# Moving the weight loads behind the first evicted keys, and reordering the first item's steps, in a block-sorted attention and mixture kernel

## The chip, the cores and the metric

The kernel runs on one core of one Trainium2 chip. The metric is device time in microseconds (us), the median of three runs. The profile is one execution of the same program; its span counts from the first to the last recorded instruction and is about 2 us shorter than the time, since it leaves out the start and the end of the launch.

## What is computed

For four batch items (B), eight heads (H), 768 positions (S) and 64 dimensions (D), the sequence is cut in 8 blocks of 96 positions. A small 8x8 matrix per head is normalised five times by rows and columns (Sinkhorn), and its rows mix the blocks of the keys and of the values. Then each block of queries attends to its own mixed block. The result, 3072 tokens of 512, goes through a layer with two first matrices whose products are compared by element, and an output matrix.

```
for _ in range(5):
    P = P - np.max(P, axis=-1, keepdims=True)
    P = np.exp(P)
    P = P / (np.sum(P, axis=-1, keepdims=True) + 1e-09)
    P = P / (np.sum(P, axis=-2, keepdims=True) + 1e-09)
k_sorted = np.einsum('bhij,bhjcd->bhicd', P, k_b)
v_sorted = np.einsum('bhij,bhjcd->bhicd', P, v_b)
scores = scale * np.matmul(q_b, k_sb.transpose(0, 1, 2, 4, 3))
attn = softmax(scores)
x = np.matmul(attn, v_sb)
out = np.maximum(x @ w1, x @ w2) @ w_out
```

The kernel uses max(a, b) = relu(a - b) + b: it forms W1 - W2 once (w_difference), computes relu(x(W1 - W2)) Wout, and adds x(W2 Wout), with the product W2 Wout computed once on the chip.

## The kernel before, in words

Each engine gets its instructions in the order in which the program text issues them, and runs them in that order. Waits between engines are semaphores that the language sets from the data. PSUM is one pool of four buffers of 4 KB per partition; every group of matmuls takes one and holds it until its eviction by VectorE (DVE) or ScalarE (ACT).

The start: TensorE (PE) runs matmuls of zeros (keep_streaming, line 82), so that its clock is up when work arrives, while DVE and ACT run the Sinkhorn rounds. There are 86 zero matmuls of 126 columns, and in the last two rounds six more of 512 columns each, which wait for a small memset of that round (late_zeros). Meanwhile GpSimd (POOL) issues all loads on one queue, with a cast from float32 to bf16: v of the first item in three pieces, k in three, q in four, then W2 and W1 by columns (lines 767 to 773), Wout, and k of the second item. An issue waits until the eighth load before it has landed. Between these POOL builds selection matrices (selections) and later computes W1 - W2 for two of the four column blocks (w_difference on lines 775 and 776); DVE does the other two (diff2 and diff3 below). ACT and DVE copy v into another order (turn_v).

Then the first item's steps, the string `front` (lines 783 to 789), is read from left to right. A step is one group of PE matmuls and its eviction:

- k0 to k2: the keys' mixing, a third each, into kT (sort_k, line 458). v0 to v3: the values' mixing, a quarter each, into v_sb (sort_v, line 479). tq0 and tq1: transposes of the queries (line 433).
- SC0 to SC7: scores of one group of heads and half the blocks (line 548), then exp on ACT into a tile e (line 556). They need all three k steps and one of the tq steps: SC0, SC1, SC4 and SC5 need tq0, the others tq1.
- VA0 to VA7: attention times values (line 575), which need that e and all four v steps; DVE then divides by the sums (lines 586 and 592) into x.
- tx0 to tx3: transposes of x (line 613). tw0 and tw1: transposes of halves of W2 (line 638). h..a and h..b: the two halves of x(W1 - W2) for a half of the tokens and a column block (line 677); the b half is evicted with the relu.
- F0 and the like: the next step's group is led by one zero matmul of 512 columns. pe2 makes the mixing matrices of the other items.

A letter at the end, A or D, fixes the engine that evicts; ACT evicts an h step without one. The first step, k0, is led by two zero matmuls of 320 columns. Behind the front come the other items, woven into the layer of the item ahead of them, and the output.

Of the kernel before, what the change touches and what calls it, by code (L numbers as in the profile page):

```python
# [11 lines left out]
BF16 = mybir.dt.bfloat16  # L12
# [4 lines left out]
def kernel(  # L17
# [16 lines left out]
    nc = tc.nc  # L34
# [4 lines left out]
    B, H, S, D = q.shape  # L39
    NB = sort_net.shape[-1]  # L40
    BLK = S // NB
    G = B * H
# [12 lines left out]
    const = ctx.enter_context(tc.tile_pool(name="const", bufs=1))  # L55
# [10 lines left out]
    def ps_f32(name):  # L66
        return psum.tile([128, 1024], FP32, tag="ps", name=name)
# [9 lines left out]
    def keep_streaming(ps, n, by=None, most=512):  # L77

        w0 = fill[:, 0:128] if by is None else late[by]
        while n > 0:  # L80
            w = min(n, most)
            nc.tensor.matmul(ps[:, 0:w], w0, fill[:, 0:w], start=True, stop=True)  # L82
            n -= w
# [35 lines left out]
    kT = {}  # L119
# [7 lines left out]
    for n in range(NE):  # L127
        t = big.tile([BLK, 8 * BLK + 32], BF16, tag=f"e{n}", name=f"e{n}")
# [23 lines left out]
    def load_k(b):  # L152
        k_raw[b] = (
            kpool.tile([128, HB * D], BF16, tag="k_raw", name="k_raw")
            if b < 3
            else v_raw[:, 0 : HB * D]
        )
        n = HB * D // NCH
        for ci in range(NCH):
            nc.gpsimd.dma_start(  # L160
                out=k_raw[b][:, ci * n : (ci + 1) * n],
                in_=k_src[b, :, ci * n : (ci + 1) * n],
            )
# [10 lines left out]
    w1_sb = big.tile([128, HP, DFF], BF16, tag="w1", name="w1_sb")  # L174
    w2_sb = big.tile([128, HP, DFF], BF16, tag="w2", name="w2_sb")
    wo_sb = big.tile([128, NFB, DMODEL], BF16, tag="wo", name="wo_sb")

    def load_w(dst, src):
        s = src.rearrange("(t p) f -> p t f", p=128)
        n = s.shape[1] // 2  # L180
        for i in range(2):
            nc.gpsimd.dma_start(
                out=dst[:, i * n : (i + 1) * n, :], in_=s[:, i * n : (i + 1) * n, :]
            )

    def load_w_columns(dst, src, t0, t1):
        s = src.rearrange("(t p) f -> p t f", p=128)
        c = slice(t0 * DFF // 4, t1 * DFF // 4)
        nc.gpsimd.dma_start(out=dst[:, :, c], in_=s[:, :, c])
# [13 lines left out]
    def selections(b, eng=nc.gpsimd):  # L203
        heads = {0: (0, 1), 2: (2, 1), 3: (3, 3)}.get(b)
        if heads:
            sel_v[b] = const.tile([G, 2, 8, NB], BF16, tag=f"sel_v{b}", name="sel_v")
            for half, item in enumerate(heads):
                eng.tensor_copy(
                    out=sel_v[b][:, half],
                    in_=ident[0:G, item * 8 : item * 8 + 8].to_broadcast([G, 8, NB]),  # L210
                )
        if b == 0:
            return
        sel_k[b] = const.tile([G, 8, 16], BF16, tag=f"sel_k{b}", name="sel_k")
        eng.tensor_copy(
            out=sel_k[b], in_=ident[0:G, b * 8 : b * 8 + 8].to_broadcast([G, 8, 16])
        )
# [11 lines left out]
    def w_difference(t, eng=None):  # L229
        n = DFF // 4  # L230
        (eng or nc.vector).tensor_tensor(
            out=w1_sb[:, :, t * n : (t + 1) * n],
            in0=w1_sb[:, :, t * n : (t + 1) * n],
            in1=w2_sb[:, :, t * n : (t + 1) * n],
            op=ALU.subtract,
        )
        if not eng:
            load["D"] += 600
# [3 lines left out]
    def turn_v(rows, eng, c0, c1):  # L242
        dst, src = v_dc[rows, 0 : D * BLK], v_raw[rows]
        if eng == "A":
            nc.scalar.copy(
                out=dst.rearrange("p (d c two) -> p d c two", c=BLK, two=2)[:, :, c0:c1],
                in_=src.rearrange("p (c d two) -> p d c two", c=BLK, two=2)[:, :, c0:c1],
            )
        else:
            nc.vector.tensor_copy(  # L250
                out=dst.bitcast(U32).rearrange("p (d c) -> p d c", c=BLK)[:, :, c0:c1],
                in_=src.bitcast(U32).rearrange("p (c d) -> p d c", c=BLK)[:, :, c0:c1],
            )
# [98 lines left out]
    def block_diagonals_first():  # L352

        pe = ps_f32("pe")
        for j in range(NB):
            nc.tensor.matmul(
                pe[:, 0:NB],
                one_j[:, j * 128 : (j + 1) * 128],
                p_bf[:, :, j],
                start=(j == 0),  # L360
                stop=(j == NB - 1),
            )
        nc.tensor.matmul(
            pe[:, 512:576],
            sel_v[0].rearrange("g two h j -> g (two h j)"),
            p_bf.rearrange("p i j -> p (i j)"),
            start=True,
            stop=True,
        )
        bd = const.tile([128, 8, NB], BF16, tag="bd10", name="bd")  # L370
        nc.vector.tensor_tensor(
            out=bd,
            in0=maskM[:, 1].to_broadcast([128, 8, NB]),
            in1=pe[:, 0:NB].to_broadcast([128, NB, 8]).transpose([0, 2, 1]),
            op=ALU.mult,
        )
        bd_k[0] = bd.rearrange("p m i -> p (m i)")
        pm = const.tile([128, NB, NB], FP32, tag="pm1", name="pm")
        nc.vector.tensor_tensor(
            out=pm,  # L380
            in0=pe[:, 512:576].rearrange("p (i j) -> p i j", j=NB),
            in1=maskJ[:, 0].to_broadcast([128, NB, NB]).transpose([0, 2, 1]),
            op=ALU.mult,
        )
        pt = const.tile([128, NB], FP32, tag="pt1", name="pt")
        nc.vector.reduce_sum(out=pt, in_=pm, axis=AX.X)
        bd = const.tile([128, 8, NB], BF16, tag="bd00", name="bd")
        nc.vector.tensor_tensor(
            out=bd,
            in0=maskM[:, 0].to_broadcast([128, 8, NB]),  # L390
            in1=pt.to_broadcast([128, NB, 8]).transpose([0, 2, 1]),
            op=ALU.mult,
        )
        bd_v[0] = bd.rearrange("p m i -> p (m i)")
# [355 lines left out]
        return SC, VA, TR  # L750

    first, second, both = slice(0, 64), slice(64, 128), slice(0, 128)
    keep_streaming(ps_f32("fill_ps"), 86 * 126, most=126)
    for it in range(5):
        sinkhorn(it)
        if it < 3:
# [5 lines left out]
    for c, n, m in [(2, 2, 0), (4, 3, 1)]:  # L762
        nc.gpsimd.tensor_copy(
            out=maskJ[:, c : c + n],
            in_=maskJ[:, m].to_broadcast([128, NB, n]).transpose([0, 2, 1]),
        )
    for t in range(2):
        load_w_columns(w2_sb, moe_w2, t, t + 1)
        load_w_columns(w1_sb, moe_w1, t, t + 1)
    for b in range(1, B):  # L770
        selections(b)
    load_w_columns(w2_sb, moe_w2, 2, 4)
    load_w_columns(w1_sb, moe_w1, 2, 4)
    load_w(wo_sb, moe_w_out)
    w_difference(0, nc.gpsimd)
    w_difference(1, nc.gpsimd)
    load_k(1)
    turn_v(first, "A", 36, 56)
    turn_v(first, "A", 56, 80)
    block_diagonals_first()  # L780
    turn_v(first, "D", 80, 96)

    front = """
        k0D k1A k2D v1D v2A v3A tq0D v0A tq1D SC1 SC0 F1
        SC2 VA1 SC5 VA0 SC3 F2 VA2 SC4 F0 tx0D SC6 VA3
        SC7 h00a VA4 tx1A tw0D h01a VA5 h01bA diff2 h00bA VA7 tx2A
        tw1A h02a VA6 h02bA h11a diff3 tx3A h12a h03a h12bD h10a h10bA
        pe2 h11bD h03bA h13a h13bA
    """.split()
    fills = [0]  # L790

# [4 lines left out]
    def front_step(step):  # L796

        eng = step[-1] if step[-1] in "AD" else None
        name = step[:-1] if eng else step
        kind = name.rstrip("0123456789ab")  # L800
        n = [int(x) for x in name if x.isdigit()]
        if kind == "F":
            fills[0] = 512
        elif kind == "k":
            sort_k(0, n[0], 640 if step == front[0] else 0, eng)
        elif kind == "v":
            sort_v(0, n[0], 0, eng)
        elif kind == "tq":
            q_transposes(0, n[0], eng)
        elif kind == "SC":  # L810
            scores(0, n[0], fills_due())
        elif kind == "VA":
            values(0, n[0], fills_due())
        elif kind == "tx":
            x_transposes(0, n[0], eng)
        elif kind == "tw":
            w2_transposes(n[0], eng)()
        elif kind == "diff":
            w_difference(n[0])
        elif kind == "pe":  # L820
            block_diagonals([(0, 2), (0, 3), (1, 1), (1, 2), (1, 3)], 2)
        elif name[-1] == "a":
            moe_h_products(0, n[0], n[1], (0, 2), fills_due())
        else:
            moe_h(0, n[0], n[1], eng, (1, 3))

    for step in front[:-26]:
        front_step(step)

    load_q(1)  # L830
# [131 lines left out]
```

The softmax here doesn't subtract the row's maximum and nothing guards it: scores larger than these inputs give would overflow.

## Time and profile before

| what | value |
|---|---|
| time, median of three (lowest, highest) | 166.7 us (166.54, 166.72) |
| span of the profile | 164.7 us |
| PE busy | 159.5 us (97%) |
| DVE, ACT, POOL busy | 76.4, 83.1, 32.7 us |
| PE idle before its first matmul | 1.2 us |
| first mixing of keys starts at | 12.21 us |
| second item's mixing of keys starts at | 38.24 us |

The share of PE tells that it is busy nearly everywhere, zero matmuls included: their 7.8 us at the start are PE time that does no work. Between the last two rows of the table stands the whole first item.

### The profile page before, as it was taken

The numbers are of one execution on the slowest core, as the hardware profiler recorded it, in microseconds if no ns is written. First come the engines' busy times: TensorE is split into PE (matmuls) and PEld (weight loads), VectorE is DVE, ScalarE is ACT, GpSimd is POOL, SyncE is SP. The second block draws the span as 40 slices with busy tenths as digits, with TensorE's granted clock in tenths as the row PEclk, the third lists the DMA queues.
The fourth block names the chain that finished last, engine by engine and source line by source line (L and its number), as shares of the span: only waits on it lengthen the run. The fifth ranks groups of instructions, "written<-read, shape, count | busy, mean of one in ns | idle before, by whom it ended". The sixth has DMA issues, their size and how long they took to land.

```text
span 164.7 us, 4563 instructions
## 1 busy us (share of the span) xinstructions
PE 159.5 (97%) x2018; PEld 96.6 (59%) x2018; DVE 76.4 (46%) x169; ACT 83.1 (50%) x102; POOL 32.7 (20%) x59
## 2 busy tenths in 40 slices
PE   7999899999999999999999999999999999999992
PEld 7958678756554555557655554575655546554451
DVE  5869778556375564535277863250642320000011
ACT  3585995918139846055652262557447206642020
POOL 7989687150104000000014010000000000000000
PEclk9999999999999999999999999999999999999999
DMA  3999999999999995688425999991025293000333
GB/s 51 200 204 197 199 208 205 210 204 220 207 205 211 218 232 108 175 116 210 98 31 97 186 193 227 184 229 12 0 52 175 50 179 128 0 0 0 127 131 128
DMA packets 30404, 23.90 MB, mean 145 GB/s; under 512 B 16752, under 2 KB 25200, under 8 KB 30384
## 3 DMA queue, kind: packets, MB, share of 16 engines
q0 software_dynamic: 11040, 13.37, 48.4%
q1 hardware_dynamic: 19200, 10.17, 26.2%
q8 instruction: 16, 0.26, 0.6%
q10 hardware_dynamic: 144, 0.07, 0.1%
q14 instruction: 4, 0.03, 0.1%
HBM read 26.75 MB, written 6.29 MB: 201 GB/s over the span
## 4 chain that ended last, share of the span: by engine, by line
PE 93%; DVE 3%; ACT 1%; issue 1%
PE out_ps L704 38%; PE h_ps L677 26%; PE fill_ps L82 6%; PE o_ps L575 5%; PE wc_ps L657 4%; PE s_ps L548 4%; PE k_ps L458 3%; PE tq_ps L433 2%; DVE kT L110 1%; PE v_ps L523 1%; PE tw_ps L638 1%; ACT e L556 1%; PE tx_ps L613 1%; PE v_ps L500 1%; DVE qT L110 1%
## 5 line engine op out<-in xcount | busy, mean ns | idle before, releaser
L704 PE MATMUL out_ps<-wo_sb,g 128*128 128x512 bf16 (+2 forms) x200 | 48.3, 371 | 0.1
L677 PE MATMUL h_ps<-xT,w_sb 128*128 128x384 bf16 x256 | 44.5, 326 | 0.0
L677 PEld LDWEIGHTS <-w_sb 128*128 128x128 bf16 x256 | 24.0, 98 | 15.6
L556 ACT ACTIVATE e<-s_ps 96x768 bf16<-96x768 f32 x32 | 23.9, 804 | 13.6 <-PE s_ps L548 13.3
L691 ACT ACTIVATE g<-h_ps 128x768 bf16<-128x768 f32 x27 | 21.8, 811 | 17.4 <-PE h_ps L677 17.3
L704 PEld LDWEIGHTS <-g 128*128 128x128 bf16 x200 | 17.1, 97 | 15.8
L704 PE MATMUL out_ps<-wc,xT 128*128 128x512 bf16 (+2 forms) x100 | 24.8, 370 | 0.0
L108 ACT COPY o<-out_ps 128x1024 f32<-128x1024 f32 x10 | 10.1, 1012 | 28.0 <-PE out_ps L704 25.2
L592 DVE TENSOR_TENSOR x<-o_ps,rs 96x512 bf16<-96x512 f32 x32 | 22.0, 687 | 1.1
L704 PEld LDWEIGHTS <-xT 128*128 128x128 bf16 x100 | 9.6, 97 | 11.2
L575 PEld LDWEIGHTS <-e 96*128 96x128 bf16 x256 | 11.8, 97 | 5.9 <-DVE v_sb L110 0.2
L586 DVE RECIPROCAL rs<-o_ps 96x8 f32<-96x8 f32 x32 | 6.4, 201 | 17.7 <-PE o_ps L575 17.5
L739 DVE COPY o<-out_ps 128x512 f32<-128x512 f32 (+1 forms) x2 | 1.2, 625 | 27.6 <-PE out_ps L704 27.6
L575 PE MATMUL o_ps<-v_sb,e 96*128 96x65 bf16 x256 | 12.9, 193 | 0.0
L110 DVE CAST kT<-k_ps 128x1024 bf16<-128x1024 f32 x7 | 8.3, 1215 | 9.4 <-PE k_ps L458 9.4
L108 ACT CAST v_sb<-v_ps 96x1024 bf16<-96x1024 f32 x10 | 9.8, 1013 | 2.5 <-PE v_ps L479 0.9
L693 DVE TENSOR_SCALAR g<-h_ps 128x768 bf16<-128x768 f32 x5 | 4.8, 956 | 10.8 <-PE h_ps L677 10.8
L110 DVE CAST v_sb<-v_ps 96x1024 bf16<-96x1024 f32 x6 | 7.3, 1217 | 5.1 <-PE v_ps L523 2.2
L160 POOL DMA_DIRECT2D v_raw<-in_k_dram x3 | 2.5, 839 | 35.2 <-DVE v_dc L250 31.4
L548 PEld LDWEIGHTS <-kT 64*128 64x128 bf16 x256 | 6.1, 94 | 5.5 <-issue 3.6
L548 PE MATMUL s_ps<-qT,kT 64*128 64x96 bf16 x256 | 8.6, 204 | 0.7 <-PE o_ps L575 0.4
L82 PE MATMUL fill_ps<-fill 128*128 128x126 bf16 x86 | 7.8, 280 | 1.2 <-DVE fill L73 1.2
(95 smaller groups left out, 143.5 us busy)
## 6 DMA issues: line engine op xcount, KB each, us to landing
out_dram<-o SPq DMA_DIRECT2D x11, 512.0 KB, 3.1
v_raw<-in_v_dram POOLq DMA_DIRECT2D x8, 384.0 KB, 12.7
k_raw<-in_k_dram POOLq DMA_DIRECT2D x9, 256.0 KB, 9.9
w_sb<-in_moe_w_dram POOLq DMA_DIRECT2D x4, 256.0 KB, 9.2
w_sb<-in_moe_w_dram POOLq DMA_DIRECT2D x2, 512.0 KB, 10.6
wo_sb<-in_moe_w_out_dram POOLq DMA_DIRECT2D x2, 512.0 KB, 14.4
v_raw<-in_v_dram POOLq DMA_DIRECT2D x3, 256.0 KB, 4.6
q_raw<-in_q_dram POOLq DMA_DIRECT2D x4, 192.0 KB, 8.8
```

The lines of the kernel that those rows point to most:

```text
L82: nc.tensor.matmul(ps[:, 0:w], w0, fill[:, 0:w], start=True, stop=True)
L108: nc.scalar.copy(out=out_ap, in_=in_ap)
L110: nc.vector.tensor_copy(out=out_ap, in_=in_ap)
L548: nc.tensor.matmul(ps[:, h2 * 512 + ii * 128 : h2 * 512 + ii * 128 + BLK], kT[b][rows, (hp * 8 + i) * BLK : (hp * 8 + i) * BLK + 128], rhs ...
L556: nc.scalar.activation(out=e[:, 0 : 8 * BLK].rearrange("p (t c r) -> p t c r", t=8, r=R), in_=ps[0:BLK] .rearrange("p (t f) -> p t f", t=8 ...
L575: nc.tensor.matmul(ps[:, h2 * 512 + ii * 65 : h2 * 512 + (ii + 1) * 65], e[:, (h2 * 4 + ii) * BLK : (h2 * 4 + ii) * BLK + 128], v_sb[:, m0 ...
L586: nc.vector.reciprocal(out=rs, in_=ov[:, :, :, 64])
L592: nc.vector.tensor_tensor(out=x, in0=ov[:, :, :, 0:D], in1=rs.to_broadcast([BLK, 2, 4, D]), op=ALU.mult,)
L657: nc.tensor.matmul(ps[:, 0:512], w2T[:, fb, dmt * 128 : (dmt + 1) * 128], wo_sb[:, fb, :], start=(fb == 0), stop=(fb == NFB - 1),)
L677: nc.tensor.matmul(h_ps[ch, t][:, m * 512 : m * 512 + TCH], w1_sb[:, hp, fb * 128 : (fb + 1) * 128], xT[:, b % 2, ch, hp % 2, hp // 2, :], ...
L691: nc.scalar.activation(out=g, in_=src, func=AF.Relu)
L704: nc.tensor.matmul(dst, g_tiles[b, ch, m // 2][:, m % 2, off : off + 128] if m < NFB else xT[:, b % 2, ch, hp % 2, hp // 2, off : off + 12 ...
```

## The change

Three things change together. The loads of W2, W1 and Wout, the two w_difference steps of POOL and the load of the second item's keys are issued on POOL only after the first piece of keys has been mixed and evicted: a two-column copy of kT into a small tile `seen` makes POOL wait for that. Another such copy, of the Sinkhorn result p_bf, stands ahead of the selection matrices of the other items, which move in front of the weight loads. The order of the first item's steps is another one, with other evicting engines and four F marks in place of three. And the zero matmuls at the start become 92 of 118 columns. The aim is to keep the weight traffic away from the loads and the engines' work that the first item needs, with an order of steps that suits the later weights.

```diff
-    keep_streaming(ps_f32("fill_ps"), 86 * 126, most=126)
+    keep_streaming(ps_f32("fill_ps"), 92 * 118, most=118)
...
-    for t in range(2):
-        load_w_columns(w2_sb, moe_w2, t, t + 1)
-        load_w_columns(w1_sb, moe_w1, t, t + 1)
-    for b in range(1, B):
-        selections(b)
-    load_w_columns(w2_sb, moe_w2, 2, 4)
-    load_w_columns(w1_sb, moe_w1, 2, 4)
-    load_w(wo_sb, moe_w_out)
-    w_difference(0, nc.gpsimd)
-    w_difference(1, nc.gpsimd)
-    load_k(1)
     turn_v(first, "A", 36, 56)
     turn_v(first, "A", 56, 80)
     block_diagonals_first()
+    seen = const.tile([128, 2, 2], BF16, tag="seen", name="seen")
+    nc.gpsimd.tensor_copy(out=seen[0:G, 0], in_=p_bf[:, NB - 1, NB - 2 :])
+    for b in range(1, B):
+        selections(b)
     turn_v(first, "D", 80, 96)
 
     front = """
-        k0D k1A k2D v1D v2A v3A tq0D v0A tq1D SC1 SC0 F1
-        SC2 VA1 SC5 VA0 SC3 F2 VA2 SC4 F0 tx0D SC6 VA3
-        SC7 h00a VA4 tx1A tw0D h01a VA5 h01bA diff2 h00bA VA7 tx2A
-        tw1A h02a VA6 h02bA h11a diff3 tx3A h12a h03a h12bD h10a h10bA
-        pe2 h11bD h03bA h13a h13bA
+        k0A k1D k2A v1A v2D v0A tq0D F0 v3D SC1 SC0 tq1D
+        SC4 F2 VA1 SC5 F1 VA0 SC3 SC2 VA4 tx0D SC7 F3
+        VA3 VA2 SC6 tw0D h00a tx1A tw1A VA5 diff3 diff2 h01a h00bA
+        h01bA tx2A h03a VA6 h03bA VA7 h02a h13a tx3D h02bD h12a h13bA
+        pe2 h12bD h10a h11a h10bA h11bA
     """.split()
...
-    for step in front[:-26]:
+    front_step(front[0])
+    nc.gpsimd.tensor_copy(out=seen[:, 1], in_=kT[0][:, 0:2])
+    for t in range(2):
+        load_w_columns(w2_sb, moe_w2, t, t + 1)
+        load_w_columns(w1_sb, moe_w1, t, t + 1)
+    load_w_columns(w2_sb, moe_w2, 2, 4)
+    load_w_columns(w1_sb, moe_w1, 2, 4)
+    load_w(wo_sb, moe_w_out)
+    w_difference(0, nc.gpsimd)
+    w_difference(1, nc.gpsimd)
+    load_k(1)
+    for step in front[1:-26]:
         front_step(step)
```

## The prediction, made before the changed kernel had run

> **What bounds the kernel now.** I read the page first. Its first part has PE busy for 97% of the span, and the chain of waits goes through PE:
>
> ```profile
> PE 159.5 (97%) x2018; PEld 96.6 (59%) x2018; DVE 76.4 (46%) x169; ACT 83.1 (50%) x102; POOL 32.7 (20%) x59
> ...
> PE 93%; DVE 3%; ACT 1%; issue 1%
> ```
>
> Asked by stretches, PE was busy 11.16 of the 12 us from 12 to 24, then 14.00 of 14 (24 to 38), 25.87 of 26 (38 to 64) and 50.00 of 50 (64 to 114). So a microsecond is won or lost only before 24 us, unless the change opens a new wait later. Then the timeline of PE, where the first item stands:
>
> ```profile
> 1.20 7.76 PE L82 MATMUL fill_ps<-fill 128*128 128x126 bf16 x86 [1.20 <-DVE fill L73]
> 8.80 2.75 PE L82 MATMUL fill_ps<-fill,late 128*128 128x512 bf16 x12
> 11.48 0.37 PE L356 MATMUL pe<-p_bf,one_j 32*128 32x8 bf16 x8
> ...
> 12.21 1.71 PE L458 MATMUL k_ps<-bd,k_raw 64*64 64x64 bf16 x96
> ...
> 18.01 0.52 PE L548 MATMUL s_ps<-qT,kT 64*128 64x96 bf16 x16
> 18.45 0.39 PE L82 MATMUL s_ps<-fill 128*128 128x512 bf16 x1
> 19.13 0.35 PE L548 MATMUL s_ps<-qT,kT 64*128 64x96 bf16 x8 [0.28 <-DVE qT L110]
> ...
> 20.25 0.34 PE L548 MATMUL s_ps<-qT,kT 64*128 64x96 bf16 x8 [0.42 <-PE o_ps L575]
> ...
> 23.56 0.82 PE L677 MATMUL h_ps<-xT,w_sb 128*128 128x384 bf16 x4
> ```
>
> The reader should see that the fills run without a gap into the first real matmul at 11.48, that the scores start at 18.01, and that two idle stretches (0.28 and 0.42 us) and the zero matmuls between the scores are what is left to win. From 23.56 on, PE has no gap until the second item at 38.24.
>
> POOL's timeline and the loads' landing times say how late the weights may be:
>
> ```profile
> 9.46 2.34 POOL L189 DMA_DIRECT2D w_sb<-in_moe_w_dram  x3
> 12.36 0.74 POOL L189 DMA_DIRECT2D w_sb<-in_moe_w_dram  x1 [0.56 <-DMA k_raw<-in_k_dram]
> ...
> 19.22 2.12 POOL L231 TENSOR_TENSOR w_sb<-w_sb 128x1024 bf16<-128x1024 bf16 x1 [1.56 <-DMA w_sb<-in_moe_w_dram]
> 21.94 2.13 POOL L231 TENSOR_TENSOR w_sb<-w_sb 128x1024 bf16<-128x1024 bf16 x1 [0.59 <-DMA w_sb<-in_moe_w_dram]
> ```
>
> The first weight load, issued at 9.46, lands 8.2 us later (17.7), while the very first load of the kernel, issued at 1.24, lands after 4.0. The other 4 us are its place in the queue: q's last piece, issued at 7.2, lands after 9.0 (16.2).
>
> **What the Trainium skill says.** "DMA: Bandwidth & Descriptors", section "Two DMAs through the same engine are not ordered", says that descriptors of one queue start in order, although they need not finish in it. The trace agrees as to landings: v, k, q, W2, W1 and Wout land in the order of issue. So weights queued behind q take nothing from q, and issuing them later should not bring q or k forward. "TensorE: Matmul & The Clock Gate", section "Back-to-back issue gap", gives N/1.2 ns for N columns while the clock is low and N/2.4 + 2.5 when it is up. For 126 columns that is 105 and 55 ns; the trace's 86 fills take 7.60 us from 1.20 to 8.80, which is 57 at 105 and 29 at 55, and the count of fills per 0.4 us indeed rises from 7 to 12 near 7.2 us. "SBUF — State Buffer", section "Who interferes with whom", says that a DVE copy in a two-port mode and a GpSimd instruction exclude each other. The turn_v copy of DVE at 12.72 (0.67 us) beside POOL's issue at 12.36 may show it, but nothing in the trace separates the two.
>
> **The change, part by part.**
>
> *Zero matmuls.* 92 of 118 columns are 10,856 columns against 10,836. If columns set the time, the clock rises again about 6.0 us after the start, 61 of them run at 98 ns and 31 at 51.7, and the end moves from 8.80 to 8.82. If each fill had a fixed price (7.60/86 = 88 ns), it would move by 6 x 88 = 0.53 us, and all of it would count, since the twelve late fills behind them end only at 11.37 while p_bf is ready at 11.07. I take 0.02: v's mixing loads 128 columns of weights per matmul of 64 and needs 34 ns per pair (48 in 1.65 us), so loading does not set the price of a fill.
>
> *Later weight loads.* POOL now waits for p_bf (11.07), copies it, makes the selections (1.6 us from 13.10 to 14.69 in the trace, now from 11.4 to 13.0), waits for kT, then issues. The k0 eviction goes to ACT, which is free at 12.21: matmuls 12.21 to 12.76, eviction 12.9 to 13.9. With the small copy the first weight issue is at 14.3 in place of 9.46. The queue has run out of q at about 14.8 and first packets follow an issue by 1.7 us (1.24 to 2.95 for v), so the queue stands empty for about 1.2 us. The first W2 piece lands between 18.3 (14.3 + 4.0) and 18.8 instead of 17.7: all weights, and everything queued behind them, come 0.6 to 1.1 us later. Six W issues of 0.74 and two Wout of 0.75 keep POOL until 20.25; its two differences end at 22.4 and 24.5 (before: 21.34 and 24.07). Who waits for them: tw0 at 23.7 needs the third piece (about 21.0 to 21.5); h00a at 24.6 needs the first difference (22.4); tw1 at 25.6 needs the fifth piece (24.3 before, now 24.9 to 25.4); diff3 on DVE at 27.8 needs the sixth (26.9 before, now 27.5 to 28.0; h03a follows at 29.1 only); h01a at 26.8 needs the second difference (24.5). Later, k of item 2 lands at 35.7 + 1.1 = 36.8 at the latest and is used from 38.2; Wout by 33.4, used at 40; the queries by 41.5, used at 43.4; the first halves of v by 45.1, used by turn_v at 45.2; the second halves by 49.2, used at 48.9, with the mixing of v at 51.8 behind a turn_v that ended at 50.42. So PE should not feel any of it, by margins of 0.2 to 2 us. I take zero; the upper end is 0.5 us if the pieces come twice as late as estimated.
>
> *The new order.* I stepped the four queues forward by hand through both strings, with the durations of the timeline: per step on PE 0.55 (k, v), 0.80 (tq), 0.22 to 0.28 (SC), 0.24 (VA, or 0.35 ahead of SC), 0.34 (tx), 0.90 (tw), 0.66 and 0.65 (h), and evictions of 1.01 and 1.22 (k, on ACT and DVE), 0.98 and 1.20 (v), 0.96 (tq), 0.81 (exp), 0.93 (reciprocal and multiply), 0.54 or 0.80 (tx), 1.23 or 1.87 (tw), 0.81 or 0.96 (h), with the four PSUM buffers as the program assigns them. For the string of before this ends the front at 38.01 (the trace: 38.24). For the new one:
>
> - k1 is evicted on DVE from 13.45 (behind turn_v), v2 from 15.1 to 16.3, tq0 from 16.6 to 17.56. So SC1 starts at 17.6, 0.4 us earlier than 18.01, and ACT, with the last v eviction done at 16.9, starts the exps at 17.9 in place of 18.39.
> - Then DVE has v3 (to 18.7) and tq1 (to 19.9) ahead of the first division: VA1 starts at 19.3 (19.41 before), VA0 with its fill waits for tq1's buffer and starts at 20.2 (20.52), tx0 waits 0.34 for the second division and starts at 21.7 (21.99).
> - VA3 with its fill waits 0.36 for the exp of SC2, the sixth in line (17.9 + 6 x 0.77 = 22.5), and starts at 22.8; VA2, SC6 and tw0 follow, h00a at 24.6.
> - From there no wait over 0.12. The front ends at 38.12.
>
> The waits and zero matmuls inside the front are 1.34 + 0.65 us in the old order and 1.42 + 0.86 in the new one; about 0.19 comes back because fewer VA groups stand ahead of an SC. Net +0.11. The score start gained is lost again at VA0, tx0 and VA3, and one more zero matmul (0.22) is paid.
>
> *The seen copies* cost POOL 0.3 us each, and POOL idles there otherwise. If a selection copy and turn_v exclude each other, turn_v ends up to 0.3 later and k1's eviction with it, which v2's (0.4 us of idle on DVE ahead of it) takes up.
>
> Sum: 0.02 + 0 + 0.11, about 0.1 us: 166.7 + 0.1 = 166.8 us.
>
> **The rivals.**
>
> 1. Faster. The pause of 0.42 us at 20.25 before has no releaser that explains it (the named o_ps group belongs to another buffer, and my stepping has SC5 at 19.8), and all of the gain of 0.4 at the scores could last until h00a if the divisions run closer than I stepped them. Against it: the new order puts 5 evictions on DVE ahead of the first division. It would give 166.7 - 0.5 = 166.2 us.
> 2. Slower, by DVE: v3 and tq1 hold back the first division, the four buffers fill, and PE waits 0.3 more at each of VA0 and tx0: 166.8 + 0.6 = 167.4 us. For it: the two longest waits I step are of this kind.
> 3. Slower, by weights: the empty queue costs 2 us in place of 1; tw1 then waits 0.7 and diff3 0.9, of which PE sees about 0.7: 167.5 us. For it: tw1's margin is 0.2 to 0.7. Against it: W's place in the queue was behind q in any case.
>
> **How the numbers follow.** No change (within 0.33 us of before) 0.41, since the sum is 0.1 and the stepping missed the known order by 0.23; rival 1 0.27; rival 2 0.2 and rival 3 0.12, together 0.32. The range runs from 165.9 (rival 1 with the second half of its reserve, another 0.3) to 167.5 (rivals 2 and 3); beyond lies the 0.53 of the fills on top of them.
>
> **What would show it.** Right: fills end within 0.05 us of 8.80; the first score at 17.5 to 17.7; the first W issue near 14.3 and the first difference near 20.3; h00a at 24.4 to 24.9; second item's k mixing at 38.2 to 38.5; PE without gaps after it. Wrong: a wait on w_sb ahead of tw1 or h01a, a late fill start near 9.3, a gap at 49 to 52 us behind turn_v, or a front that ends before 37.9 or after 38.6.

## The result and the profile after

| what | before | after |
|---|---|---|
| time, median (lowest, highest) | 166.62 us (166.15, 166.72) | 167.52 us (167.21, 167.77) |
| span of the profile | 164.7 us | 165.8 us |
| first mixing of keys starts at | 12.21 us | 11.93 us |
| second item's mixing of keys starts at | 38.24 us | 39.29 us |
| from there to the end of the span | 126.46 us | 126.51 us |

The changed kernel takes 1.0059 times as long, with a 95% interval of 1.0033 to 1.0085: it is slower by 0.9 us, where the forecast was no change. The last row tells where to look. What follows the second item's first matmul is as long as before, so all of the loss lies in the first 39 us.

The page of the changed kernel, its busy times and then its chain of waits (shares of the span), answers the first lines shown of the kernel before:

```profile
PE 159.4 (96%) x2025; PEld 96.4 (58%) x2025; DVE 77.3 (47%) x170; ACT 82.4 (50%) x101; POOL 33.3 (20%) x61
...
PE 82%; DMA 7%; DVE 5%; POOL 2%; ACT 2%; issue 1%
PE out_ps L704 37%; PE h_ps L677 25%; DMA w_sb<-in_moe_w_dram 6%; PE wc_ps L657 4%; PE o_ps L575 4%; PE k_ps L458 3%; PE s_ps L548 3%; POOL w_sb L189 2%; PE v_ps L523 1%; DMA p_sb<-in_sort_net_dram 1%; DVE v_dc L250 1%; PE tq_ps L433 1%; DVE colsum L276 1%; DVE p_sb L273 1%; PE tw_ps L638 1%
```

PE's work is the same to 0.1 us, but PE's share of the chain fell from 93% to 82%, and the DMA of w_sb, which had no part that was shown before, now has 6%, with POOL's issues of it at 2% (L189). Somewhere the weights have become the last to arrive. The timeline of PE (start, duration, group, and in brackets the idle time and its releaser) says where:

```profile
1.20 7.31 PE L82 MATMUL fill_ps<-fill 128*128 128x118 bf16 x92 [1.20 <-DVE fill L73]
8.34 2.75 PE L82 MATMUL fill_ps<-fill,late 128*128 128x512 bf16 x12
...
11.93 1.84 PE L458 MATMUL k_ps<-bd,k_raw 64*64 64x64 bf16 x96
...
17.29 0.52 PE L548 MATMUL s_ps<-qT,kT 64*128 64x96 bf16 x16 [0.16 <-DVE qT L110]
...
24.13 0.81 PE L677 MATMUL h_ps<-xT,w_sb 128*128 128x384 bf16 x4
24.78 0.51 PE L613 MATMUL tx_ps<-ident,x 96*128 96x96 bf16 x8
26.76 1.07 PE L638 MATMUL tw_ps<-ident,w_sb 128*128 128x128 bf16 x16 [1.48 <-DMA w_sb<-in_moe_w_dram]
...
39.29 1.70 PE L458 MATMUL k_ps<-bd,k_raw 64*64 64x64 bf16 x96
```

The line of 26.76 is tw1, the transposes of the second half of W2. PE stands still for 1.48 us ahead of it, for the fifth piece of the weights, the second half of W2. Up to there the new order is no worse than the old: the scores start at 17.29 in place of 18.01, the bracket of 0.42 us at 20.25 is gone, and h00a runs at 24.13, where I had stepped 24.6.

Of the 0.72 us at the scores, 0.28 is the earlier first mixing, which differs as much between profiles with the same zero matmuls. These 92 zero matmuls took 7.31 us here, and 7.78 and 6.25 in two of the experiments below (tw1 put later, and the new order with the loads at their old place):

```profile
1.20 7.78 PE L82 MATMUL fill_ps<-fill 128*128 128x118 bf16 x92 [1.20 <-DVE fill L73]
1.20 6.25 PE L82 MATMUL fill_ps<-fill 128*128 128x118 bf16 x92 [1.20 <-DVE fill L73]
```

In the six profiles with this form, one matmul takes 99 ns at first and 52 later, and the step comes at 3.9 us in one profile and at 7.2 in another. The first mixing starts between 11.90 and 12.21 us accordingly, so a difference of 0.3 us in a single pair of profiles tells nothing of the kernels.

POOL's timeline answers the lines shown of before and tells why the piece is late:

```profile
11.23 0.18 POOL L771 COPY seen<-p_bf 32x2 bf16<-32x2 bf16 x1 [1.76 <-DVE p_bf L278]
...
13.73 0.19 POOL L821 COPY seen<-kT 128x2 bf16<-128x2 bf16 x1 [0.49 <-ACT kT L108]
13.97 4.45 POOL L189 DMA_DIRECT2D w_sb<-in_moe_w_dram  x6
18.37 1.53 POOL L182 DMA_DIRECT2D wo_sb<-in_moe_w_out_dram  x2
21.24 2.12 POOL L231 TENSOR_TENSOR w_sb<-w_sb 128x1024 bf16<-128x1024 bf16 x1 [1.34 <-DMA w_sb<-in_moe_w_dram]
```

The first issue comes at 13.97 in place of 9.46, close to the 14.3 of the prediction. By the trace, the first weight piece then lands at 19.08 (before: 17.69), the third at 22.45 (20.51), the fifth at 26.71 (24.34) and the sixth at 29.32 (26.94). The last piece of q had landed at 16.86 (16.36). The delay is 1.4 us at the first piece, 2.0 at the second (21.10 in place of 19.08) and 2.4 from the fifth on, so most of it is made before 21 us. The two kernels by stretches (busy time and count of each engine, then PE's clock, the packets in flight on the DMA engines, as a multiple of their number of sixteen, and KB moved per us), first before:

```profile
15.00:16.00 1.00, 0.96 (x30) 0.79 (x28) 1.00 (x2) 0.76 (x1) 1.00 (x2) 1.00 1.43 197
16.00:17.00 1.00, 1.00 (x36) 0.91 (x33) 1.00 (x2) 1.00 (x2) 1.00 (x3) 1.00 1.44 195
17.00:18.00 1.00, 1.00 (x34) 0.86 (x30) 0.72 (x1) 0.83 (x2) 0.66 (x1) 1.00 1.50 210
18.00:19.00 1.00, 0.84 (x21) 0.56 (x18) 0.88 (x1) 0.94 (x2) 0.00 (x0) 1.00 1.40 187
19.00:20.00 1.00, 0.70 (x16) 0.49 (x15) 0.21 (x2) 1.00 (x3) 0.78 (x1) 1.00 1.47 196
```

and after:

```profile
15.00:16.00 1.00, 1.00 (x33) 0.88 (x31) 1.00 (x1) 1.00 (x2) 1.00 (x2) 1.00 0.75 101
16.00:17.00 1.00, 1.00 (x27) 0.69 (x21) 0.80 (x2) 0.65 (x1) 1.00 (x3) 1.00 1.27 170
17.00:18.00 1.00, 0.84 (x27) 0.73 (x28) 1.00 (x2) 0.33 (x1) 1.00 (x2) 1.00 0.89 90
18.00:19.00 1.00, 1.00 (x31) 0.74 (x26) 0.72 (x2) 1.00 (x2) 1.00 (x2) 1.00 1.16 137
19.00:20.00 1.00, 1.00 (x23) 0.72 (x22) 0.97 (x3) 1.00 (x3) 0.91 (x2) 1.00 1.09 132
```

The last column is the one to read. Before, these five microseconds move 985 KB (197 + 195 + 210 + 187 + 196). After, they move 630 KB. The missing 355 KB are 1.8 us of transfer at 197 KB per us. Only a part of it is the empty queue that I had foreseen. From 15 to 16 us, where q runs out and the first weight packets come (15.42), 96 KB are missing. From 17 to 20 us 234 KB are missing: the rate is 90 to 137 there, and the packets in flight are 0.89 to 1.16 in place of 1.40 to 1.50.

### The profile page after: what moved, and what is told of

The parts are those of the page before. It is cut to its first block, busy times and chain, and to the rows that moved or that the text cites. A ratio compares the mean times of both kernels' runs of the same rounds, so it can differ in the third digit from the quotient of the medians.

```text
span 165.8 us, 4579 instructions
## 1 busy us (share of the span) xinstructions
PE 159.4 (96%) x2025; PEld 96.4 (58%) x2025; DVE 77.3 (47%) x170; ACT 82.4 (50%) x101; POOL 33.3 (20%) x61
## 4 chain that ended last, share of the span: by engine, by line
PE 82%; DMA 7%; DVE 5%; POOL 2%; ACT 2%; issue 1%
PE out_ps L704 37%; PE h_ps L677 25%; DMA w_sb<-in_moe_w_dram 6%; PE wc_ps L657 4%; PE o_ps L575 4%; PE k_ps L458 3%; PE s_ps L548 3%; POOL w_sb L189 2%; PE v_ps L523 1%; DMA p_sb<-in_sort_net_dram 1%; DVE v_dc L250 1%; PE tq_ps L433 1%; DVE colsum L276 1%; DVE p_sb L273 1%; PE tw_ps L638 1%
## 5 line engine op out<-in xcount | busy, mean ns | idle before, releaser
L677 PEld LDWEIGHTS <-w_sb 128*128 128x128 bf16 x256 | 24.0, 98 | 15.5
L110 DVE CAST kT<-k_ps 128x1024 bf16<-128x1024 f32 x6 | 7.2, 1222 | 10.0 <-PE k_ps L458 9.9
L110 DVE CAST v_sb<-v_ps 96x1024 bf16<-96x1024 f32 x7 | 8.5, 1219 | 4.8 <-PE v_ps L523 2.8
L108 ACT CAST v_sb<-v_ps 96x1024 bf16<-96x1024 f32 x9 | 8.8, 1009 | 1.4 <-PE v_ps L500 0.8
L169 POOL DMA_DIRECT2D v_raw<-in_v_dram x11 | 5.9, 541 | 13.3 <-DVE v_dc L250 7.7
## 6 DMA issues: line engine op xcount, KB each, us to landing
v_raw<-in_v_dram POOLq DMA_DIRECT2D x8, 384.0 KB, 14.3
```

The source lines that it names most:

```text
L108: nc.scalar.copy(out=out_ap, in_=in_ap)
L110: nc.vector.tensor_copy(out=out_ap, in_=in_ap)
L169: nc.gpsimd.dma_start(out=v_raw[r0 : r0 + 64, m * n : (m + 1) * n], in_=v_src[b, :, m * n : (m + 1) * n],)
L677: nc.tensor.matmul(h_ps[ch, t][:, m * 512 : m * 512 + TCH], w1_sb[:, hp, fb * 128 : (fb + 1) * 128], xT[:, b % 2, ch, hp % 2, hp // 2, :], ...
```

## The experiments

Two questions stood open. First, is the wait of tw1 the whole loss, and does it come from the place of the loads or from the order of the steps? I call the theory that the loads' place alone loses the time W; its rivals lay it on the order or on the zero matmuls. Second, what was the pause of 0.42 us at 20.25, which is gone in the changed kernel? Each ratio below is against the kernel before, with its 95% interval.

**The new order with the loads at their old place.** The changed kernel, with the loads, selections and differences put back at their old place and neither of the two copies:

```diff
+    for t in range(2):
+        load_w_columns(w2_sb, moe_w2, t, t + 1)
...
     turn_v(first, "A", 36, 56)
...
     front_step(front[0])
-    nc.gpsimd.tensor_copy(out=seen[:, 1], in_=kT[0][:, 0:2])
-    for t in range(2):
-        load_w_columns(w2_sb, moe_w2, t, t + 1)
...
```

> The changed kernel with the weight loads, differences and selections back at their old place on GpSimd (first W issue near 9.5 us); new order of steps and 92 x 118 zero matmuls kept. Theory W (the late weights cost it all): the 1.48 us wait ahead of tw1 goes, and with it the loss; 167.5 - 1.4 = 166.1 us, second item's keys at about 37.8 us. Rival O (the new order is itself slower, the wait only uncovers what VectorE would hold up anyway): no faster than before, 166.7 to 167.2 us.

Measured: 166.6 us, 1.0001 (0.9976 to 1.0026). The wait is gone (tw1 at 25.63, the fifth piece lands at 24.34 as before) and so is the loss. But nothing is won either, and PE's timeline shows why:

```profile
19.55 0.39 PE L575 MATMUL o_ps<-v_sb,e 96*128 96x65 bf16 x7 [0.51 <-issue]
...
25.63 1.06 PE L638 MATMUL tw_ps<-ident,w_sb 128*128 128x128 bf16 x16
```

The pause is back, 0.51 us long, in the middle of a group of eight (the first matmul of VA1 had gone ahead). In the old order it stood before a score. A wait for data would not move from a score to attention times values; the trace names no releaser for it.

**The old order with the late loads.** The kernel before, with both copies and the moved loads and selections, its own order and zero matmuls:

```diff
-    for t in range(2):
-        load_w_columns(w2_sb, moe_w2, t, t + 1)
...
+    nc.gpsimd.tensor_copy(out=seen[0:G, 0], in_=p_bf[:, NB - 1, NB - 2 :])
...
+    front_step(front[0])
+    nc.gpsimd.tensor_copy(out=seen[:, 1], in_=kT[0][:, 0:2])
...
```

> The kernel before with only the weight loads, differences and selections moved behind the first evicted keys, which in the old order VectorE evicts later (14.5 us). Theory W: weights land 2.5 to 3.2 us later; h00a and h01a wait for the differences of GpSimd (0.6 and 1.2 us), diff2 on VectorE for the last W1 piece; 166.6 + 1.3 = 167.9 us (167.4 to 168.3). Rival O: the old order hides late weights, as tw1 comes at 28.5 only; 166.6 us.

Measured: 167.68 us, 1.0069 (1.0042 to 1.0096). The loss comes with the loads alone. In this order it shows as other waits, by PE's timeline:

```profile
25.84 0.82 PE L677 MATMUL h_ps<-xT,w_sb 128*128 128x384 bf16 x4 [0.20 <-POOL w_sb L231]
...
30.36 0.82 PE L677 MATMUL h_ps<-xT,w_sb 128*128 128x384 bf16 x4 [0.67 <-DVE w_sb L231]
```

h01a waits for POOL's second difference and h02a for the difference on DVE, both of which wait for a weight piece. The pause at 20.25 is absent here.

**The zero matmuls alone.**

```diff
-    keep_streaming(ps_f32("fill_ps"), 86 * 126, most=126)
+    keep_streaming(ps_f32("fill_ps"), 92 * 118, most=118)
```

> The kernel before with 92 zero matmuls of 118 columns alone. If columns set their time: end of the fills near 8.8 us, 166.6 us, no change. If the 8.34 us of the changed kernel's profile comes from the form of the fills: fills end near 8.3, 0.3 us faster, 166.3 us. If each fill has a fixed price: 167.1 us.

Measured: 166.43 us, 0.9973 (0.9954 to 0.9993). Columns set the price: a fixed price per fill would have cost 0.53 us. The gain of 0.4 us by the median ratio I can't explain; the profile of this kernel still has the pause (0.44 us).

**The changed kernel without the copy of kT.** The loads then wait for the Sinkhorn result alone:

```diff
-    nc.gpsimd.tensor_copy(out=seen[:, 1], in_=kT[0][:, 0:2])
```

> The changed kernel without the copy that waits for the evicted keys: the weight loads are issued behind p_bf and the selections, near 12.9 us in place of 13.97. Theory W with an emptied queue as the cause: the first packets of W come just as q runs out (14.8 us), no lull in the queue, W lands within 0.5 us of before, no wait ahead of tw1; 166.1 to 166.3 us. Rival: each us of later issue costs a us of landing, queue empty or not; tw1 waits about 0.4 us, 166.6 us.

Measured: 166.26 us, 0.9961 (0.9943 to 0.9979). This version beats both kernels. First POOL, then PE from its timeline:

```profile
12.72 4.53 POOL L189 DMA_DIRECT2D w_sb<-in_moe_w_dram  x6
```

```profile
24.05 0.81 PE L677 MATMUL h_ps<-xT,w_sb 128*128 128x384 bf16 x4
24.70 0.51 PE L613 MATMUL tx_ps<-ident,x 96*128 96x96 bf16 x8
25.04 1.06 PE L638 MATMUL tw_ps<-ident,w_sb 128*128 128x128 bf16 x16
```

and its stretches:

```profile
15.00:16.00 1.00, 1.00 (x32) 0.87 (x28) 0.99 (x1) 1.00 (x2) 1.00 (x3) 1.00 1.46 213
16.00:17.00 1.00, 1.00 (x23) 0.65 (x18) 0.81 (x1) 0.57 (x1) 1.00 (x2) 1.00 1.33 163
17.00:18.00 1.00, 0.84 (x29) 0.78 (x30) 1.00 (x2) 0.41 (x1) 1.00 (x3) 1.00 1.43 180
```

In this profile an issue 1.25 us earlier (12.72 against 13.97) brings the fifth piece 1.95 us earlier (24.76 against 26.71): the queue still holds a part of q when the first weights join it, and the rate never falls below 163. tw1 follows tx1 with no wait, and the second item's keys start at 37.55 in place of 39.29. From the start of tx1 to that of tw1 the changed kernel takes 1.98 us, this one 0.34. (The bracket of 1.48 is smaller than these 1.64, as it counts from the modelled end of tx1.) With the 0.08 by which PE comes earlier to tx1 here, that is 1.72 of the 1.74: PE passes the wait on in full. By the medians the two kernels are 1.3 us apart, since the profiled run of this one, of 165.88 us, was a short one.

**tw1 put later.** The changed kernel, with tw1 behind the second half of h01:

```diff
-        VA3 VA2 SC6 tw0D h00a tx1A tw1A VA5 diff3 diff2 h01a h00bA
-        h01bA tx2A h03a VA6 h03bA VA7 h02a h13a tx3D h02bD h12a h13bA
+        VA3 VA2 SC6 tw0D h00a tx1A VA5 diff3 diff2 h01a h00bA
+        h01bA tw1A tx2A h03a VA6 h03bA VA7 h02a h13a tx3D h02bD h12a h13bA
```

> The changed kernel with the step tw1 moved from ahead of VA5 to behind h01b, where its piece of W2 (landing at 26.7 us) has come. Theory W (the whole stream of weights is 2.4 us late): other steps wait in tw1's place, h01a for GpSimd's second difference (ends 26.0, about 0.6 us) and h03a for diff3 (last W1 piece lands at 29.3, about 0.9 us), so 167.3 to 167.6 us, next to no gain. Rival T (only tw1 stands too early in the new order): the 1.48 us go, 166.1 us.

Measured: 167.58 us, 1.0058 (1.0038 to 1.0077). Nothing is won. PE's timeline has two other waits in place of the one:

```profile
26.07 2.13 PE L677 MATMUL h_ps<-xT,w_sb 128*128 128x384 bf16 x12 [0.39 <-POOL w_sb L231]
...
29.75 0.82 PE L677 MATMUL h_ps<-xT,w_sb 128*128 128x384 bf16 x4 [0.32 <-DVE w_sb L231]
```

Not one piece is late, the stream is. The two brackets sum to 0.71 us, but from start to start, against the kernel without the copy of kT, these two steps come 0.55 and 0.49 us later after the step ahead of them, 1.04 together. Another 0.29 comes at 31.83, in a wait for DVE's division that the other kernel does not have. That is the 1.3 us by which the first item is longer here (12.21 to 39.13, against 11.91 to 37.55).

**Larger pieces.** The changed kernel, with the first two pieces of each matrix as one load, whose packets are of 1 KB in place of 512 B:

```diff
-    for t in range(2):
-        load_w_columns(w2_sb, moe_w2, t, t + 1)
-        load_w_columns(w1_sb, moe_w1, t, t + 1)
+    load_w_columns(w2_sb, moe_w2, 0, 2)
+    load_w_columns(w1_sb, moe_w1, 0, 2)
```

> The changed kernel, still gated by the evicted keys, with the first halves of W2 and W1 in one load of 512 columns each (1 KB packets) in place of two of 256 (512 B packets). If small packets behind an emptied queue make the slow refill from 15 to 20 us: the fifth piece of before lands about 1 us earlier (25.7), tw1 waits about 0.5 us, 166.6 us. If the empty time alone makes it: lands at 26.5, 167.4 us.

Measured: 167.05 us, 1.0026 (1.0006 to 1.0046), half of the loss. The first issue is at 13.96, as in the changed kernel, but from 17 to 20 us the DMA engines move 196, 193 and 185 KB per us where they moved 90, 137 and 132. W2's second half lands at 25.53 in place of 26.71, and tw1 waits for nothing. h00a waits for POOL's first difference, which now needs a larger piece:

```profile
25.12 0.82 PE L677 MATMUL h_ps<-xT,w_sb 128*128 128x384 bf16 x4 [0.61 <-POOL w_sb L231]
```

POOL issues here until 18.4, so issuing alone does not slow the transfers; the size of the packets has a part in it. That the queue had run short before them is not a full account, as the next experiment shows.

**The old order with the copy of p_bf alone.** The kernel before, with the loads behind the first copy only (as the second experiment, without the line of kT):

> The kernel before with the weight loads issued behind p_bf and the selections (12.7 us), old order and old zero matmuls. Theory I (weights queued early hold back the fetch of PE's own instructions, which shows as the pause of 0.42 us behind PE matmul 351): the fetch starts at about 15 to 16 us in place of 17.8, the pause goes, 166.7 - 0.3 = 166.4 us. Rival (the pause belongs to the order, not to the loads): pause and time stay, 166.7 us.

Measured: 166.58 us, 0.9998 (0.998 to 1.0016). Against the second experiment only the copy of kT is missing, and the loss with it. So that copy makes the loss in the old order too, and the moved selections and the copy of p_bf cost nothing.

The pause stays, 0.44 us, which the expectation had going. That the loads are later is not enough. And the rate falls here as well, although the first weight issue is at 12.72 and the queue still held work (183 KB per us from 15 to 16 us):

```profile
17.00:18.00 1.00, 1.00 (x36) 0.86 (x34) 0.60 (x2) 0.83 (x2) 1.00 (x3) 1.00 1.46 154
18.00:19.00 1.00, 0.71 (x19) 0.43 (x17) 0.93 (x1) 0.94 (x3) 0.74 (x1) 1.00 0.92 119
```

The fifth piece lands at 25.79, 1.0 us later than in the version of the new order with the same first issue. An early gate brings the weights earlier, but not by a fixed amount, and it does not keep the rate up by itself.

**Fewer zero matmuls.** The version without the copy of kT, with less of them, since the scores had come early:

```diff
-    keep_streaming(ps_f32("fill_ps"), 92 * 118, most=118)
+    keep_streaming(ps_f32("fill_ps"), 80 * 118, most=118)
...
-        SC4 F2 VA1 SC5 F1 VA0 SC3 SC2 VA4 tx0D SC7 F3
+        SC4 F2 VA1 SC5 F1 VA0 SC3 SC2 VA4 tx0D SC7
```

> The kernel that waits for p_bf alone (new order, weights issued at 12.7 us), with 80 zero matmuls of 118 columns and without the mark F3. Fills no longer end behind p_bf (11.1 us) in any run: 0 to 0.3 us; one zero matmul less where PE is the bound: 0.2 us. 166.26 - 0.3 = 166.0 us (165.7 to 166.2). Leaves out work that has no part in the output.

Measured: 169.49 us in six runs of 168.44 to 170.91, 1.0162 (1.0104 to 1.0219): far slower, with less work to do. PE's timeline has two pauses that nothing releases:

```profile
15.47 0.87 PE L479 MATMUL v_ps<-bd,v_dc 64*128 64x64 bf16 x24 [1.05 <-issue]
...
22.49 0.26 PE L548 MATMUL s_ps<-qT,kT 64*128 64x96 bf16 x3 [1.76 <-issue]
```

Counted from 0 in the program's matmuls (the traces of the experiments lack one late zero matmul, which is counted in), the first stands ahead of number 223 and the second ahead of number 351, 128 apart. The pauses of the other kernels (before, the first and third experiments, the old order with p_bf alone) all stand ahead of number 351 too, whatever the step there. The changed kernel's page has a queue that fits, in its part on DMA queues (packets, MB, share of the sixteen engines' span):

```profile
q8 instruction: 16, 0.26, 0.7%
```

I read these 16 packets of 16 KB as PE's own program: its 2025 matmuls and as many weight loads are 253 instructions per packet, so blocks of 256 fit, and 256 instructions are 128 matmuls, the distance of the pauses. The theory that I call I: PE's next block is fetched over the same DMA engines as the loads, and where many loads are queued it comes late. It asks for the block at the boundary before, 128 matmuls earlier. Two tests follow: as many zero matmuls but narrower, and the kernel before with fewer but wider ones.

```diff
-    keep_streaming(ps_f32("fill_ps"), 80 * 118, most=118)
+    keep_streaming(ps_f32("fill_ps"), 92 * 108, most=108)
```

> The kernel that waits for p_bf alone, with 92 zero matmuls of 108 columns (same number of instructions, 920 columns fewer) and without the mark F3. Theory I (what hurt the kernel with 80 zero matmuls is where PE's instruction fetches fall, 128 matmuls apart, not less warming): no pause behind matmuls 223 and 351, fills end by 8.3 us, 0.2 us less from F3, 166.0 us (165.7 to 166.2). Rival (shorter warming, or F3 left out, made the 1.05 and 1.76 us pauses): 168 us or more. Leaves out zero matmuls, which have no part in the output.

```diff
-    keep_streaming(ps_f32("fill_ps"), 86 * 126, most=126)
+    keep_streaming(ps_f32("fill_ps"), 80 * 135, most=135)
```

> The kernel before with 80 zero matmuls of 135 columns in place of 86 of 126: 36 columns fewer of 10,836, six matmuls fewer. Theory I: the fetch that is asked for at matmul 95 is asked for about 1 us later (matmul 95 now stands behind p_bf), into a queue full of loads, and PE pauses behind matmul 223 (about 1 us) and 351 (0.5 to 1.8 us); 168.0 to 169.5 us. Rival (columns alone count): 166.6 us, no change.

Measured: the narrow ones 166.25 us, 0.998 (0.9969 to 0.9991), without any such pause; its profile has tw1 waiting 0.5 us, for a fifth piece at 25.68, with a first issue at 13.20 and rates of 123 and 107 KB per us from 17 to 19 us. The wide ones 168.21 us, 1.0101 (1.0064 to 1.0139), though 10,800 columns are 36 fewer than before. The second one's timeline of PE:

```profile
15.68 0.87 PE L479 MATMUL v_ps<-bd,v_dc 64*128 64x64 bf16 x24 [0.62 <-issue]
...
21.88 0.22 PE L548 MATMUL s_ps<-qT,kT 64*128 64x96 bf16 x2 [1.03 <-issue]
```

Both again ahead of numbers 223 and 351. So the count of zero matmuls, and not their columns, brings the pauses. With 80 of them the boundary before, at number 95, lies behind the zero matmuls, in the work that waits for the Sinkhorn result: PE passes it at 11.3 and 11.6 us in these two kernels, in the others between 8.7 and 10.9. The packets of the instruction queue in the trace, for the block that begins at 351:

| kernel | PE passes number 223 | packet starts, ends | delay | pause ahead of 351 |
|---|---|---|---|---|
| before | 14.63 | 17.83, 18.81 | 3.2 | 0.42 |
| new order, old place of loads | 13.89 | 17.23, 18.19 | 3.3 | 0.51 |
| old order, copy of p_bf alone | 14.5 | 17.82, 18.80 | 3.3 | 0.44 |
| before with 80 wide fills | 15.7 | 19.47, 20.45 | 3.8 | 1.03 |
| 80 fills, no copy of kT | 15.5 | 19.92, 20.81 | 4.4 | 1.76 |
| zero matmuls alone | 14.46 | 17.58, 18.56 | 3.1 | 0.44 |
| 92 narrow fills, no copy of kT | 14.11 | 16.95, 17.91 | 2.8 | 0.1 at most |
| no copy of kT | 13.98 | 15.93, 16.89 | 1.9 | none |
| after | 14.07 | 15.47, 16.44 | 1.4 | none |
| old order, late loads | 14.63 | 14.89, 16.11 | 0.3 | none |

Where there is a pause, it ends 1.3 to 1.7 us after the packet (before: 20.25 - 18.81 = 1.44). With 92 narrow fills PE comes to the boundary 1.3 us after the packet, just in time. The first and the last row have the same order and zero matmuls and differ in the place of the loads: with the weights behind it the packet starts 0.3 us after the boundary in place of 3.2, and the pause is gone. Elsewhere too the packet is late where the weights are queued early or the boundary is passed late. That the block is asked for at the boundary before fits all ten rows, but is inferred; no record shows the asking. (The two kernels that are not listed, with tw1 put later and with larger pieces, have delays of 1.0 and 1.1 and no pause.) Nor is it settled why the packet starts at 17.82 in the old order with p_bf alone and at 15.93 in the new one, with the first weight issue at 12.72 in both: PE passes number 223 half a microsecond later there, when more weights are queued.

## Why the prediction was wrong

- **Zero matmuls, +0.02: right.** Alone they cost nothing (0.9973). That their number also shifts where the blocks of PE's program begin was in no step.
- **First weight issue at 14.3, the queue then empty: right in the main** (13.97; first packets at 15.42). The queue ran short rather than empty, as q's last piece landed at 16.86. The 1.7 us from an issue to its first packet was misread: v's first packet starts at 2.60 and not at 2.95, 1.36 us after its issue; here it is 1.45.
- **"All weights, and everything queued behind them, come 0.6 to 1.1 us later": this step failed.** They came 1.4 us later at the first piece and 2.4 at the fifth. I had counted the time in which the queue is empty, and let it go on at full rate after that. It went on at 90 to 137 KB per us from 17 to 20 us. The experiment with larger pieces shows the weight of this second part: with the same gate, W2's second half is 1.2 us earlier. Why the rate falls is open.
- **"So PE should not feel any of it ... I take zero": it failed with it.** The same list of needs had tw1 at 25.6 with the fifth piece due by 25.4 at the latest. With 26.71 in its place it gives a wait of 1.1; measured were 1.48, since PE had come to tw1 earlier, at 25.3. The margins of "0.2 to 2 us" were not those of the list either: v's first halves have 0.1 there and its second halves less than nothing (49.2, needed at 48.9). The mechanism was that of rival 3, to which I gave 0.12 and which had the queue cost 2 us and tw1 wait 0.7. Its own size was half of what came. The counterweight that I named, that the weights stand behind q in any case, tells of the order and nothing of the rate.
- **The new order, +0.11: the forecast of "about even" held, the parts did not.** With the loads at their old place, order and zero matmuls together are even (1.0001). Without the copy of kT they come to 0.9961, some 0.65 us of 166.6, and no fetch pauses PE. How much of that is the order's own is not shown, since the zero matmuls alone gave 0.9973 with an interval that holds 0.9961. In the changed kernel's profile the first item, from its first mixing of keys to the second item's, takes 1.33 us longer than before: the wait, 1.64 from start to start, less about 0.3 won ahead of it. The earlier first mixing takes off 0.28 more, which leaves the 1.05 of the table's fourth row.
- **"Weights queued behind q take nothing": it fell.** I had concluded it from the Trainium skill, "DMA: Bandwidth & Descriptors", section "Two DMAs through the same engine are not ordered", which says only that within one queue of one DMA engine descriptors start in order. That still agrees with the landings, which follow the order of issue in all kernels here. But my conclusion looked at loads alone. In the kernel before, the packet that I read as PE's program starts 3.2 us after the boundary, and 0.3 with the weights issued late. The pause of 0.42 us, of which rival 1 said that no releaser explains it, goes with it.
- **From the second item on, no change: right** (126.46 and 126.51 us), although v lands at 45.3 to 50.59 us, up to 3 us later than before.

Open: what gives the zero matmuls alone 0.4 us, and why the rate falls for some microseconds behind a gate, early or late. In the changed kernel it is back (189 from 20 to 22 us) when POOL's last weight issue has ended, at 19.9, and in the old order with the copy of p_bf alone likewise (186 from 19 us on, last issue until 18.7). Whether the two are linked was not tested.

## What to carry to other kernels

When loads are held back behind a gate, look at the rate of the queue behind it and not only at the time of issue. Here the kernels whose gate opened while the queue still held q lost nothing by it (0.9961, 0.998, 0.9998; with 80 zero matmuls the pauses cost their time apart from it), and those with the later gate did (1.0026 to 1.0069). But the landing did not follow the issue by a fixed time: with the first issue at 12.72 in both orders, the fifth piece came at 24.76 in one and at 25.79 in the other. Moving one consumer back won nothing, because the whole stream was late. Compare waits from start to start, and do not trust 0.3 us between two single profiles. A pause of an engine with no releaser that moves from step to step but keeps the same number in the program can be the fetch of its instructions; compare it with the packets of the instruction queue. Then even work that is free, such as zero matmuls, has a price by its count, and queued loads have one before any of their data is needed.

## What the runs showed of the hardware

- Pauses of PE of 0.42 to 1.76 us without a releaser stood 128 matmuls apart, and each ended 1.3 to 1.7 us after a packet of 16 KB of the instruction queue. Read as PE's program, such a packet started 0.3 us after the boundary before it ahead of the weights, and 3.1 to 4.4 us after it where a pause followed.
- Weights in packets of 512 B moved at 187 to 210 KB per us in the kernel before, which issues its first at 9.46. Behind a gate the rate fell to 90 to 137 for three microseconds (copy of kT), or to 119 and 107 in its lowest (copy of p_bf, old order, and 92 narrow fills), but not under 163 in one profile with the copy of p_bf. Packets of 1 KB behind the copy of kT moved at 185 to 196.
- The same row of zero matmuls went from 99 to 52 ns each at 3.9 us in one profile and at 7.2 in another.
